# A sketched-attention plus squared-ReLU feed-forward kernel: the first 512 tokens as two chunks of 256, and 256-token chunks in blocks of two w_in tiles

## The chip, the cores and the metric

The kernel runs on one core of one Trainium2 chip. The metric is device microseconds (us) of one execution. Before the change three runs gave 219.83, 217.87 and 219.4 us, a median of 219.4. The core's engines have these names in the profile: PE multiplies matrices (PEld is its loading of weights), DVE, ACT and POOL work on vectors, SP only issues DMAs here. All engines run side by side, each through its own queue in order, and wait for each other at semaphores.

## The reference

Four batches, four heads, 1088 positions, head size 32. The attention is linear: a feature map phi of 64 products replaces the softmax.

```python
def phi(x):
    a = np.einsum('rd,bhsd->bhsr', S1, x)      # r = 8
    b = np.einsum('rd,bhsd->bhsr', S2, x)
    return np.einsum('bhsi,bhsj->bhsij', a, b).reshape(*x.shape[:-1], r * r)
q_p, k_p = (phi(q), phi(k))
kv  = np.einsum('bhsf,bhsd->bhfd', k_p, v)
z   = np.sum(k_p, axis=2)
num = np.einsum('bhsf,bhfd->bhsd', q_p, kv)
den = np.einsum('bhsf,bhf->bhs', q_p, z)[..., None] + 1e-06
x   = (num / den)          # -> (4352 tokens, 128)
h   = np.maximum(x @ w_in, 0.0)       # w_in  (128, 2048)
out = h * h @ w_out                   # w_out (2048, 128)
```

All inputs and the output are float32.

## The kernel before, in words

**Tokens and chunks.** Each batch has 1024 main positions, read as 128 partitions by 8 positions, and 64 remaining ones. The main positions make two groups of 512 tokens (`g` = 0 and 1, four tiles of 128); the remainders of all four batches make one chunk of 256 tokens. So the feed-forward part has nine chunks: eight of 512 tokens and, in seventh place counted from nought, the remainder chunk of 256.

**Attention part of one group.** `proj_t` (line 187) transposes the four heads of a group on PE and evicts them (tile `xt`), `proj` (203) multiplies by the sketches (`ab_ps`, evicted to `ab`) and forms the outer products `ph`, two tiles of 128 tokens at a time (line 221). `Kv` (237) sums keys times values into `kv_ps`, with the remainder's keys last (`finish`, line 263), and evicts the two halves of `kvbd`. For the queries, `feature_t` (295) transposes `ph` in two sets of four (one per pair of heads) and evicts each (`phT`), `numerators` (308) multiplies by `kvbd` into `nd`, `normalize` (319) is a chain of nine DVE instructions from `nd` to `xs` plus one on POOL (`beta`), then transposes on PE (`x_ps`) and an ACT copy to `xT`, float16. `xT` scales each token so that it fits float16, and `beta`, the squared scale, is multiplied in at the end.

**Feed-forward part.** A chunk has 16 blocks, one per tile of 128 columns of `w_in`. A block is: first product `pg` on PE (line 534, float16), ReLU on ACT to `gt` (537), square on DVE to `g2` (538), second product on PE into `po` (554, float32, which PE runs as two instructions). `first_product` runs `LOOK` = 2 blocks ahead of `block`. `pg` has two PSUM buffers. The last chunk (`LAST` = 8) multiplies the other way round (563), so that its tokens need no transposing; each other chunk is transposed back (`o_ps`, 497) and stored by a DMA on SP's queue.

**What sets the order.** `start` (586) is written by hand under `manual_schedule`: every engine runs it in program order. It makes batch 0's keys, its values' sums, the queries of group 0 as far as the first chunk, and the queries of group 1 (`second`, a `q_gen`) as far as their outer products. In it are `idle_products` (150), multiplications of zeros that nothing uses, and the four ACT casts of `w_in` to float16 (616). The remainder's projection `ph_krem[0]` (606) stands ahead of the sums. After `by_hand.close()` the instructions are ordered by a planner, which takes program order as priority and lets later instructions through where earlier ones are not ready by its own costs. Program order there comes from the loop at line 632: after each block `pump(2)` advances up to two lanes of side work (`q_gen`, `k_gen`, remainder), and each `yield n` in a lane says how many blocks it rests. A chunk's first product must come after its `xT` in program order.

Of the kernel before, what the change touches and what calls it, by code (L numbers as in the profile page):

```python
# [8 lines left out]
F32 = mybir.dt.float32  # L9
F16 = mybir.dt.float16  # L10
# [11 lines left out]
def kernel(  # L22
# [11 lines left out]
    nc = tc.nc  # L34

    B, H, S, D = 4, 4, 1088, 32
    DFF, NC = 2048, 16
# [90 lines left out]
    q_sb[1] = load(q, 1, "q_sb")  # L128


    zero = cpool.tile([128, 128], F32)
    nc.vector.memset(zero[:], 0.0)
    iden = cpool.tile([128, 128], F32)
    make_identity(nc, iden[:])
# [12 lines left out]
        nc.vector.memset(_v(v_rem[i], D, [[VW, H]]), 1.0)  # L147
        nc.vector.memset(_v(v_main[i], D, [[VW, H * NJ]]), 1.0)

    def idle_products(n):  # L150
        idle_ps = pspool.tile([128, 512], F32, name="idle_ps", tag="po", bufs=2)
        for i in range(n):
            nc.tensor.matmul(idle_ps[:, 0:128], zero[:, :], zero[:, :])

    idle_products(6)
    w_in = cpool.tile([128, DFF], F16)

    def spread_v(b, eng, j0=0, w=NJ, heads=range(H), pin=False):
# [41 lines left out]
        evict(eng, xt[:, 0 : 128 * n], xt_ps[:, 0 : 128 * n])  # L200
        return xt

    def proj(xt, T, tag, eng, outer, ps_tag="ms", m=32):

        n = 4 if T == 4 else 1
        ab_ps = pspool.tile([128, 256], F32, tag=ps_tag, bufs=2)
        for i in range(n):
            tiled(ab_ps, 64 * i, 64, xt, 128 * i, w_bd[:, :], m=m)
        ab = apool.tile([128, 256], F32, tag="ab", bufs=3)
        if T == 4:  # L210
            evict(
                eng,
                _v(ab, 0, [[16, 4], [64, 4], [1, 16]]),
                _v(ab_ps, 0, [[64, 4], [16, 4], [1, 16]]),
            )
        else:
            evict(eng, ab[:, 0:64], ab_ps[:, 0:64])
        ph = apool.tile([128, 1024], F32, tag=tag, bufs=3)
        for t0 in range(0, T, 2):
            m = min(2, T - t0)  # L220
            outer[(t0 // 2) % len(outer)].tensor_tensor(  # L221
                out=_v(ph, 256 * t0, [[64, 4 * m], [8, 8], [1, 8]]),
                in0=_v(ab, 64 * t0, [[16, 4 * m], [1, 8], [0, 8]]),
                in1=_v(ab, 64 * t0 + 8, [[16, 4 * m], [0, 8], [1, 8]]),
                op=mult,
            )
        return ph

    ph_krem = {}

# [74 lines left out]
        evict(eng, sb[:, 0 : 128 * T], t_ps[:, 0 : 128 * T])  # L305
        return sb

    def numerators(b, phT, m):
        nd = pspool.tile([128, 1024], F32, name="nd", tag="nd", bufs=1)
        for t in range(4):  # L310
# [67 lines left out]
    def chunk_of(b, g, xT, beta):  # L378
        dst = bass.AP(out.tensor, out.offset + (b * S + 4 * g) * E, [[NJ * E, 128], [1, 512]])
        chunks.append((xT, 4, [(beta, 4)], [(dst, 0, 128, 0, 512)]))  # L380

    def x_gen(b, g, phT, m=32):
        nd = numerators(b, phT, m)
# [135 lines left out]
            nc.sync.dma_start(dst, _v(o_sb, c0, [[1, w]], p0, n))  # L519

    LOOK = 2
    LAST = 8
    stream = []
    made = [0]

    def first_product():

        ci, c = divmod(made[0], NC)
        if ci >= len(chunks):
            return False  # L530
        xT, T, _, _ = chunks[ci]
        nt = 128 * T
        pg = pspool.tile([128, 512], F32, tag="pg", bufs=2)
        nc.tensor.matmul(pg[:, 0:nt], w_in[:, 128 * c : 128 * c + 128], xT[:, 0:nt])  # L534
        gt = fpool.tile([128, 512], F32, tag="gt")
        g2 = fpool.tile([128, 512], F32, tag="g2")
        nc.scalar.activation(gt[:, 0:nt], pg[:, 0:nt], Relu)  # L537
        nc.vector.tensor_tensor(  # L538
            out=g2[:, 0:nt], in0=gt[:, 0:nt], in1=gt[:, 0:nt], op=mult
        )  # L540
        stream.append((ci, c, nt, g2))
        made[0] += 1
        return True

    po = [None]
# [1 line left out]
    def block():  # L547
        while len(stream) <= LOOK and first_product():
            pass
        ci, c, nt, g2 = stream.pop(0)  # L550
        if c == 0:
            po[0] = pspool.tile([128, 512], F32, name="po", tag="po", bufs=2)
        if ci < LAST:
            nc.tensor.matmul(  # L554
                po[0][:, 0:nt], w_o[:, 128 * c : 128 * c + 128], g2[:, 0:nt],
                start=(c == 0), stop=(c == NC - 1),
            )
        else:

            for t in range(nt // 128):
                nc.tensor.matmul(  # L563
                    po[0][:, 128 * t : 128 * t + 128],
                    g2[:, 128 * t : 128 * t + 128],
                    w_o[:, 128 * c : 128 * c + 128],
                    start=(c == 0 and t == 0), stop=(c == NC - 1),
                    skip_group_check=True,
                )
        now[0] += 1  # L570
        if c == NC - 1:
# [14 lines left out]
    def start():  # L586
        s_ps = pspool.tile([128, 16], F32, name="s_ps", tag="po", bufs=2)
        xk = [proj_t(k_sb[0], 0, 4, act)]
        nc.tensor.transpose(s_ps[:, :], s_nat[:, :], iden[0:16, 0:16])
        for h in range(H):  # L590
            nc.vector.tensor_copy(
                out=_v(w_bd, 16 * h, [[1, 16]], 32 * h, 32),
                in_=_v(s_ps, 0, [[1, 16]], 32 * h, 32),
            )
        xk.append(proj_t(k_sb[0], 1, 4, act))
        idle_products(2)
        pk = [proj(x, 4, "ph_k", act, (dve,), "pg", m=64) for x in xk]
        idle_products(1)
        xq = proj_t(q_sb[0], 0, 4, act)
        spread_v(0, act, 0, 4)  # L600
        pq = proj(xq, 4, "ph_q", act, (dve,), "pg", m=64)
        xkr = proj_t(k_rm[0], 0, 1, act)
        spread_v(0, act, 4, 4, (0, 1))
        spread_v(0, pool, 4, 4, (2, 3))
        spread_vrem(0, pool)
        ph_krem[0] = proj(xkr, 1, "ph_kr", act, (dve,), "pg", m=64)
        kv0 = Kv(0, 64, "po", 2)
        kv0.tiles(pk[0], 0, range(4))
        pqT = [feature_t(pq, 4, 0, act)]
        kv0.tiles(pk[1], 1, range(4))  # L610
        pqT.append(feature_t(pq, 4, 1, act))
        kv0.finish((dve, dve))
        first = x_gen(0, 0, pqT, 64)
        next(first)
        for c in range(4):
            act.copy(
                w_in[:, 512 * c : 512 * c + 512], w_in32[:, 512 * c : 512 * c + 512]
            )
        for _ in range(3):
            next(first)  # L620
        second = q_gen(0, 1, (dve,), 64)
        next(second)
        idle_products(3)
        next(second)
        idle_products(4)
        whole(first)
        return second

    second = start()
    by_hand.close()  # L630
# [1 line left out]
    for b in range(B):  # L632
# [25 lines left out]
            pump(2)  # L658
        if b + 1 < B:
            drain()  # L660
    for c in range(NC):
        block()
        pump_stores()
        pump(2)
# [31 lines left out]
```

## Time and profile before

| what | value |
|---|---|
| runs | 219.83, 217.87, 219.4 us; median 219.4 |
| the profiled execution | 217.62 us in all, span of its instructions 215.8 us |
| granted PE clock over the span | 0.997 |
| first instruction of the first chunk's first product | 20.15 us |
| DVE busy | 144.3 us (67%) |
| ACT busy | 119.1 us (55%) |
| POOL busy | 44.8 us (21%) |
| squares on DVE, 128x512 | 128 of them, 776 ns mean |
| squares on DVE, 128x256 (remainder chunk) | 16 of them, 424 ns mean |
| ReLU on ACT, 128x512 and 128x256 | 600 and 384 ns mean |

The profile gives each engine's instructions with their start and duration. A matmul's start and end are modelled, and successive matmuls overlap, so that the pitch between two equal ones, not the duration of one, is what one costs. A note in square brackets behind a row is idle time before it and what ended that. Times inside the profile count from the start of the span.

### The profile page before, as it was taken

To read this page: it belongs to the slowest core of one execution; us is meant where nothing else is said; L and a number is where in the kernel's file an instruction comes from. 1 tells how busy PE (TensorE), PEld (TensorE's weight loads), DVE (VectorE), ACT (ScalarE), POOL (GpSimd) and SP (SyncE) were. 2 spreads that over 40 slices of the span, in tenths; PEclk is the share of its full clock that TensorE was granted. 3 is DMA by queue.
4 is the path that set the end of the run, shared out by engine and by line. 5 is a ranking of instruction groups with operands and counts; after the bars stand their busy time and mean duration, and the time that the engine had idled before them with its cause. 6 is when DMAs were issued, how large, how long until landed. Compare 5 with 4: busy or idle time off the path is not lost.

```text
span 215.8 us, 5391 instructions
## 1 busy us (share of the span) xinstructions
PE 207.4 (96%) x2253; PEld 125.4 (58%) x2253; DVE 144.3 (67%) x279; ACT 119.1 (55%) x234; POOL 44.8 (21%) x59
## 2 busy tenths in 40 slices
PE   8889999999999999999999999999999899999992
PEld 7677545445545664655546565455545454669992
DVE  2637696658685799557775567657868777677661
ACT  3655654564566555556466663656465456665550
POOL 1302273004050672004120960013101200000000
PEclk9999999999999999999999999999999999999998
DMA  6999900001000460001000100000000000100001
GB/s 172 270 312 319 267 8 3 2 3 49 3 0 0 131 212 3 3 0 52 2 0 0 52 3 2 3 16 36 2 3 19 30 5 0 49 0 15 12 0 49
DMA packets 13575, 11.35 MB, mean 53 GB/s; under 512 B 3824, under 2 KB 11760, under 8 KB 13552
## 3 DMA queue, kind: packets, MB, share of 16 engines
q1 hardware_dynamic: 12928, 10.95, 17.0%
q8 instruction: 17, 0.28, 0.5%
q10 hardware_dynamic: 624, 0.07, 0.2%
q14 instruction: 6, 0.05, 0.1%
HBM read 8.79 MB, written 2.23 MB: 51 GB/s over the span
## 4 chain that ended last, share of the span: by engine, by line
PE 86%; DVE 6%; ACT 1%; issue 1%; DVEq 0%
PE po L554 46%; PE pg L534 14%; PE po L563 7%; PE nd L180 5%; PE t_ps L299 4%; PE kv_ps L249 3%; PE xt_ps L194 3%; PE ab_ps L180 2%; PE o_ps L497 2%; DVE g L538 1%; DVE xs L358 1%; PE x_ps L370 1%; DVE o_sb L511 1%; DVE small L339 1%; ACT xt L59 1%
## 5 line engine op out<-in xcount | busy, mean ns | idle before, releaser
L538 DVE TENSOR_TENSOR g<-gt 128x512 f32<-128x512 f32 (+1 forms) x144 | 104.8, 737 | 50.5 <-ACT gt L537 48.5
L554 PE MATMUL po<-g,w_o 128*128 128x512 f32 (+1 forms) x256 | 124.1, 570 | 1.1 <-DVE g L538 1.1
L537 ACT ACTIVATE gt<-pg 128x512 f32<-128x512 f32 (+1 forms) x144 | 82.6, 576 | 48.2 <-PE pg L534 47.4
L554 PEld LDWEIGHTS po<-g,w_o 128*128 128x128 f32 x256 | 46.7, 191 | 27.8 <-DVE g L538 9.6
L534 PE MATMUL pg<-xT,w_in 128*128 128x512 f16 x128 | 48.6, 381 | 0.1
L221 POOL TENSOR_TENSOR ph<-ab 128x512 f32<-128x512 f32 (+1 forms) x27 | 32.1, 1213 | 69.7 <-ACT ab L59 69.6
L534 PEld LDWEIGHTS <-w_in 128*128 128x128 f16 x144 | 14.2, 99 | 17.7 <-issue 15.0
L59 ACT COPY sb<-t_ps 128x512 f32<-128x512 f32 (+1 forms) x20 | 10.3, 521 | 12.9 <-PE t_ps L299 12.9
L563 PEld LDWEIGHTS po<-w_o,g 128*128 128x128 f32 x128 | 16.3, 192 | 0.8 <-DVE g L538 0.4
L563 PE MATMUL po<-w_o,g 128*128 128x128 f32 x128 | 16.4, 275 | 0.0
L59 ACT COPY xt<-xt_ps 128x512 f32<-128x512 f32 (+1 forms) x20 | 10.3, 524 | 7.1 <-PE xt_ps L194 7.0
L364 POOL TENSOR_TENSOR beta<-mp 128x4 f32<-128x4 f32 (+1 forms) x10 | 3.1, 319 | 52.3 <-DVE mp L346 44.4
L59 ACT COPY ab<-ab_ps 128x256 f32<-128x256 f32 (+1 forms) x20 | 6.8, 340 | 13.0 <-PE ab_ps L180 12.5
L180 PEld LDWEIGHTS nd<-kvbd,sb 128*32 128x32 f32 (+1 forms) x512 | 8.9, 111 | 7.3 <-issue 3.2
L299 PEld LDWEIGHTS t_ps<-iden,ph 128*128 128x128 f32 x68 | 8.4, 141 | 8.0 <-issue 4.9
L180 PE MATMUL ab_ps<-w_bd,xt 128*32 128x64 f32 (+1 forms) x476 | 11.6, 223 | 1.1 <-ACT xt L59 1.1
L180 PEld LDWEIGHTS ab_ps<-w_bd,xt 128*32 128x32 f32 (+1 forms) x476 | 8.7, 113 | 6.5 <-ACT gt L537 3.0
L180 PE MATMUL nd<-kvbd,sb 128*32 128x66 f32 (+1 forms) x512 | 10.8, 222 | 0.7 <-DVE kvbd L60 0.7
L299 PE MATMUL t_ps<-iden,ph 128*128 128x128 f32 x68 | 10.9, 276 | 0.2 <-DVE ph L221 0.2
L194 PEld LDWEIGHTS xt_ps<-iden,t 128*128 128x128 f32 x52 | 6.4, 141 | 5.2 <-issue 2.8
L194 PE MATMUL xt_ps<-iden,t 128*128 128x128 f32 x52 | 8.3, 276 | 0.1
L249 PEld LDWEIGHTS kv_ps<-v_main,ph 128*32 128x32 f32 (+1 forms) x448 | 5.7, 113 | 2.7 <-issue 0.9
(57 smaller groups left out, 115.6 us busy)
## 6 DMA issues: line engine op xcount, KB each, us to landing
out_dram<-o_sb SPq DMA_DIRECT2D x8, 256.0 KB, 2.0
t<-in_k_dram SPq DMA_DIRECT2D x3, 512.0 KB, 6.5
t<-in_v_dram SPq DMA_DIRECT2D x3, 512.0 KB, 7.5
t<-in_q_dram SPq DMA_DIRECT2D x3, 512.0 KB, 7.3
w_in<-in_moe_w_in_dram SPq DMA_DIRECT2D x2, 512.0 KB, 6.0
k_sb<-in_k_dram SPq DMA_DIRECT2D x2, 256.0 KB, 3.1
q_sb<-in_q_dram SPq DMA_DIRECT2D x2, 256.0 KB, 5.7
v_sb<-in_v_dram SPq DMA_DIRECT2D x2, 256.0 KB, 5.6
```

The lines of the kernel that those rows point to most:

```text
L59: return nc.scalar.copy(dst, src)
L180: nc.tensor.matmul(out_ps[p0 + c : p0 + c + m, c0 : c0 + w], lhsT[:, l0 + c : l0 + c + m], rhs,)
L194: nc.tensor.transpose(xt_ps[:, 128 * i : 128 * i + 128], src[:, w * i + 128 * g : w * i + 128 * g + 128], iden[:, :],)
L221: outer[(t0 // 2) % len(outer)].tensor_tensor(out=_v(ph, 256 * t0, [[64, 4 * m], [8, 8], [1, 8]]), in0=_v(ab, 64 * t0, [[16, 4 * m], [1, 8 ...
L249: nc.tensor.matmul(self.ps[c : c + self.m, VW * pr : VW * pr + VW], _v(ph, c0 + 128 * pr + c, [[1, self.m]], p0, n), _v(vt, v0 + VW * (2 * ...
L299: nc.tensor.transpose(t_ps[:, 128 * t : 128 * t + 128], ph[:, 256 * t + 128 * pr : 256 * t + 128 * pr + 128], iden[:, :],)
L497: nc.tensor.transpose(o_ps[:, 128 * t : 128 * t + 128], oT[:, 128 * t : 128 * t + 128], iden[:, :])
L534: nc.tensor.matmul(pg[:, 0:nt], w_in[:, 128 * c : 128 * c + 128], xT[:, 0:nt])
L537: nc.scalar.activation(gt[:, 0:nt], pg[:, 0:nt], Relu)
L538: nc.vector.tensor_tensor(out=g2[:, 0:nt], in0=gt[:, 0:nt], in1=gt[:, 0:nt], op=mult)
L554: nc.tensor.matmul(po[0][:, 0:nt], w_o[:, 128 * c : 128 * c + 128], g2[:, 0:nt], start=(c == 0), stop=(c == NC - 1),)
L563: nc.tensor.matmul(po[0][:, 128 * t : 128 * t + 128], g2[:, 128 * t : 128 * t + 128], w_o[:, 128 * c : 128 * c + 128], start=(c == 0 and t ...
```

## The change

- The first group of 512 tokens becomes two chunks of 256 (`half_gen`, `half_features_t`). The first half's features are transposed alone, four transposes with one eviction; the second half's are transposed after the four casts of `w_in`, in the hand-written part. The second half's numerators and normalization move out of `start` to the head of the first lane of the loop, with `second` behind them (`rest`).
- `proj` can leave outer products out (`only`); the second half's outer product is issued after the remainder's.
- The remainder's projection stands behind the first half of the keys' sums, no longer ahead of all.
- `kv0.finish` evicts one half of `kvbd` on DVE and one on ACT, where both were on DVE.
- A chunk of 256 tokens takes two tiles of `w_in` in one block: two first products side by side in one `pg`, one ReLU and one square over 512 columns, two second products. This holds for the two new chunks and for the remainder chunk.
- There are ten chunks, so `LAST` is 9; the closing loop runs until nothing is left.
- `zero` is 512 columns wide, and idle products are given by widths: 384+384 in place of six of 128 at the beginning, 256 for two, 128 for one, and one of 384 ahead of the first chunk where there were three and four of 128.

```diff
-    zero = cpool.tile([128, 128], F32)
+    zero = cpool.tile([128, 512], F32)
...
-    def idle_products(n):
+    def idle_products(*widths):
         idle_ps = pspool.tile([128, 512], F32, name="idle_ps", tag="po", bufs=2)
-        for i in range(n):
-            nc.tensor.matmul(idle_ps[:, 0:128], zero[:, :], zero[:, :])
-
-    idle_products(6)
+        for w in widths:
+            nc.tensor.matmul(idle_ps[:, 0:w], zero[:, 0:128], zero[:, 0:w])
+
+    idle_products(384, 384)
...
+    def half_features_t(ph, t0, eng):
+
+        t_ps = pspool.tile([128, 512], F32, name="t_ps", tag="ms", bufs=2)
+        for pr in range(2):
+            for t in range(2):
+                nc.tensor.transpose(
+                    t_ps[:, 256 * pr + 128 * t : 256 * pr + 128 * t + 128],
+                    ph[:, 256 * (t0 + t) + 128 * pr : 256 * (t0 + t) + 128 * pr + 128],
+                    iden[:, :],
+                )
+        sb = apool.tile([128, 512], F32, name="phT_h", tag=f"phT{t0 // 2}")
+        evict(eng, sb[:, :], t_ps[:, :])
+        return [sb[:, 256 * pr : 256 * pr + 256] for pr in range(2)]
...
+    def half_gen(phT, t0, m):
+
+        nd = numerators(0, phT, m, 2)
+        yield 1
+        xT = apool.tile([128, 256], F16, name="xT_h", tag=f"xT_h{t0}", bufs=1)
+        beta = yield from normalize(nd, 2, xT, 0)
+        dst = bass.AP(out.tensor, out.offset + t0 * E, [[NJ * E, 128], [1, 256]])
+        chunks.append((xT, 2, [(beta, 2)], [(dst, 0, 128, 0, 256)]))
+        yield 1
...
-    LAST = 8
+    LAST = 9
...
+        n = 4 // T
         pg = pspool.tile([128, 512], F32, tag="pg", bufs=2)
-        nc.tensor.matmul(pg[:, 0:nt], w_in[:, 128 * c : 128 * c + 128], xT[:, 0:nt])
+        for i in range(n):
+            nc.tensor.matmul(
+                pg[:, nt * i : nt * i + nt],
+                w_in[:, 128 * (c + i) : 128 * (c + i) + 128],
+                xT[:, 0:nt],
+            )
...
-        nc.scalar.activation(gt[:, 0:nt], pg[:, 0:nt], Relu)
-        nc.vector.tensor_tensor(
-            out=g2[:, 0:nt], in0=gt[:, 0:nt], in1=gt[:, 0:nt], op=mult
-        )
+        nc.scalar.activation(gt[:, :], pg[:, :], Relu)
+        nc.vector.tensor_tensor(out=g2[:, :], in0=gt[:, :], in1=gt[:, :], op=mult)
...
+        for i in range(n):
+            c = c0 + i
+            if ci < LAST:
                 nc.tensor.matmul(
+                    po[0][:, 0:nt], w_o[:, 128 * c : 128 * c + 128],
+                    g2[:, nt * i : nt * i + nt],
+                    start=(c == 0), stop=(c == NC - 1),
                 )
...
-        idle_products(2)
+        idle_products(256)
         pk = [proj(x, 4, "ph_k", act, (dve,), "pg", m=64) for x in xk]
-        idle_products(1)
+        idle_products(128)
         xq = proj_t(q_sb[0], 0, 4, act)
         spread_v(0, act, 0, 4)
-        pq = proj(xq, 4, "ph_q", act, (dve,), "pg", m=64)
+        pq = proj(xq, 4, "ph_q", act, (dve,), "pg", m=64, only=(0,))
         xkr = proj_t(k_rm[0], 0, 1, act)
...
-        ph_krem[0] = proj(xkr, 1, "ph_kr", act, (dve,), "pg", m=64)
         kv0 = Kv(0, 64, "po", 2)
         kv0.tiles(pk[0], 0, range(4))
-        pqT = [feature_t(pq, 4, 0, act)]
+        ph_krem[0] = proj(xkr, 1, "ph_kr", act, (dve,), "pg", m=64)
+        outer_of(*pq, 2, dve)
         kv0.tiles(pk[1], 1, range(4))
-        pqT.append(feature_t(pq, 4, 1, act))
-        kv0.finish((dve, dve))
-        first = x_gen(0, 0, pqT, 64)
+        pqT = half_features_t(pq[1], 0, act)
+        kv0.finish((dve, act))
+        first = half_gen(pqT, 0, 64)
         next(first)
...
         for _ in range(3):
             next(first)
+        pqT = half_features_t(pq[1], 2, act)
         second = q_gen(0, 1, (dve,), 64)
         next(second)
-        idle_products(3)
         next(second)
-        idle_products(4)
+        idle_products(384)
         whole(first)
-        return second
+
+        def rest():
+            yield from half_gen(pqT, 2, 64)
+            yield from second
+
+        return rest()
...
-    for c in range(NC):
+    while made[0] < len(chunks) or stream or lanes:
         block()
```

More of the change, by code (lines that the diff above doesn't have):

```diff
@@ L201, in proj_t, with outer_of, proj @@
         return xt
-    def proj(xt, T, tag, eng, outer, ps_tag="ms", m=32):
+    def outer_of(ab, ph, t0, eng, m=2):
+        eng.tensor_tensor(
+            out=_v(ph, 256 * t0, [[64, 4 * m], [8, 8], [1, 8]]),
+            in0=_v(ab, 64 * t0, [[16, 4 * m], [1, 8], [0, 8]]),
+            in1=_v(ab, 64 * t0 + 8, [[16, 4 * m], [0, 8], [1, 8]]),
+            op=mult,
+        )
+    def proj(xt, T, tag, eng, outer, ps_tag="ms", m=32, only=None):
         n = 4 if T == 4 else 1
@@ L218, in proj @@
         ph = apool.tile([128, 1024], F32, tag=tag, bufs=3)
[L219 to L225, printed above, removed]
-            )
-        return ph
+        for t0 in range(0, T, 2) if only is None else only:
+            outer_of(ab, ph, t0, outer[(t0 // 2) % len(outer)], min(2, T - t0))
+        return ph if only is None else (ab, ph)
     ph_krem = {}
@@ L306, in feature_t, with numerators @@
         return sb
-    def numerators(b, phT, m):
+    def half_features_t(ph, t0, eng):
[10 more added lines that the diff above has]
+        return [sb[:, 256 * pr : 256 * pr + 256] for pr in range(2)]
+    def numerators(b, phT, m, T=4):
         nd = pspool.tile([128, 1024], F32, name="nd", tag="nd", bufs=1)
-        for t in range(4):
+        for t in range(T):
             for pr in range(2):
@@ L521 @@
     LOOK = 2
-    LAST = 8
+    LAST = 9
     stream = []
-    made = [0]
+    made = [0, 0]
     def first_product():
-        ci, c = divmod(made[0], NC)
+        ci, c = made
         if ci >= len(chunks):
@@ L532, in first_product @@
         nt = 128 * T
+        n = 4 // T
         pg = pspool.tile([128, 512], F32, tag="pg", bufs=2)
-        nc.tensor.matmul(pg[:, 0:nt], w_in[:, 128 * c : 128 * c + 128], xT[:, 0:nt])
+        for i in range(n):
[3 more added lines that the diff above has]
+                xT[:, 0:nt],
+            )
         gt = fpool.tile([128, 512], F32, tag="gt")
         g2 = fpool.tile([128, 512], F32, tag="g2")
-        nc.scalar.activation(gt[:, 0:nt], pg[:, 0:nt], Relu)
-        nc.vector.tensor_tensor(
-            out=g2[:, 0:nt], in0=gt[:, 0:nt], in1=gt[:, 0:nt], op=mult
-        )
-        stream.append((ci, c, nt, g2))
-        made[0] += 1
+        nc.scalar.activation(gt[:, :], pg[:, :], Relu)
+        nc.vector.tensor_tensor(out=g2[:, :], in0=gt[:, :], in1=gt[:, :], op=mult)
+        stream.append((ci, c, n, nt, g2))
+        made[:] = (ci, c + n) if c + n < NC else (ci + 1, 0)
         return True
@@ L549, in block @@
             pass
-        ci, c, nt, g2 = stream.pop(0)
-        if c == 0:
+        ci, c0, n, nt, g2 = stream.pop(0)
+        if c0 == 0:
             po[0] = pspool.tile([128, 512], F32, name="po", tag="po", bufs=2)
[L553 to L562, printed above, removed]
-                nc.tensor.matmul(
[L564 to L568, printed above, removed]
-                )
+        for i in range(n):
+            c = c0 + i
+            if ci < LAST:
+                nc.tensor.matmul(
+                    po[0][:, 0:nt], w_o[:, 128 * c : 128 * c + 128],
+                    g2[:, nt * i : nt * i + nt],
+                    start=(c == 0), stop=(c == NC - 1),
+                )
+            else:
+                for t in range(nt // 128):
+                    nc.tensor.matmul(
+                        po[0][:, 128 * t : 128 * t + 128],
+                        g2[:, 128 * t : 128 * t + 128],
+                        w_o[:, 128 * c : 128 * c + 128],
+                        start=(c == 0 and t == 0), stop=(c == NC - 1),
+                        skip_group_check=True,
+                    )
         now[0] += 1
-        if c == NC - 1:
+        if c0 + n == NC:
             if ci < LAST:
```

## Prediction

> **What bounds the kernel now.** I read the page first: its busy times, its clock row and its chain of waits.
>
> ```profile
> PE 207.4 (96%) x2253; PEld 125.4 (58%) x2253; DVE 144.3 (67%) x279; ACT 119.1 (55%) x234; POOL 44.8 (21%) x59
> PEclk9999999999999999999999999999999999999998
> PE 86%; DVE 6%; ACT 1%; issue 1%; DVEq 0%
> ```
>
> PE bounds the kernel at full clock. The change takes almost no work from PE: it multiplies the same columns. So the time can only move by what PE spends on nothing useful: the start, where it waits or multiplies zeros, and later bubbles. The start needs the timeline from 14 to 21 us (start, duration, engine, line, operation, count, idle before).
>
> ```profile
> 14.08 0.58 ACT L59 COPY sb<-t_ps 128x512 f32<-128x512 f32 x1 [1.06 <-PE t_ps L299]
> 14.56 2.18 ACT L616 CAST w_in<-w_in 128x512 f16<-128x512 f32 x4
> 15.05 1.16 PE L180 MATMUL nd<-kvbd,sb 128*64 128x66 f32 x32 [0.66 <-DVE kvbd L60]
> 16.84 0.59 ACT L59 COPY xt<-xt_ps 128x512 f32<-128x512 f32 x1
> 17.48 0.69 PE L180 MATMUL ab_ps<-w_bd,xt 128*64 128x64 f32 x16
> 18.09 1.16 PE L153 MATMUL idle_ps<-zero 128*128 128x128 f32 x8
> 18.33 0.69 DVE L358 TENSOR_TENSOR xs<-nd,small 128x512 f16<-128x512 f32 x1
> 19.09 0.40 PE L370 MATMUL x_ps<-iden,xs 128*128 128x128 f16 x4
> 19.52 0.58 ACT L373 COPY xT<-x_ps 128x512 f16<-128x512 f16 x1 [0.89 <-PE x_ps L370]
> 20.15 0.59 PE L534 MATMUL pg<-xT,w_in 128*128 128x512 f16 x2
> ```
>
> Two chains meet at 19.1: the numerators and nine DVE instructions (15.05 to 19.02), and ACT's queue: casts, `xt`, then PE's `ab_ps` and the idle products that stand before `x_ps`. The reader is to see that they are level, so that shortening one alone gains nothing. Third, the table of stretches behind the first chunk's beginning (PE, PEld, DVE, ACT, POOL busy, clock, DMA).
>
> ```profile
> 24.00:26.00 2.00, 2.00 (x22) 1.20 (x24) 0.42 (x1) 1.56 (x3) 0.00 (x0) 1.00 1.10 258
> 30.00:32.00 2.00, 1.99 (x39) 0.76 (x27) 1.93 (x6) 0.89 (x2) 1.71 (x4) 1.00 0.00 0
> 32.00:34.00 2.00, 1.85 (x53) 0.78 (x49) 2.00 (x3) 0.81 (x2) 2.00 (x2) 1.00 0.00 0
> ```
>
> DVE is full from 28 to 34 us, while POOL forms batch 1's outer products: normalization and squares share DVE. PE looks busy, but the chain of waits runs over DVE from 27.05 to 32.56 (5.5 us); PE's work in it, four first products, three second and 0.85 of side work by pitch, is 4.9. So 0.6 us is lost, hidden by modelled ends.
>
> **The change part by part.**
>
> *The start of PE.* `zero` quadruples. DVE memsets of 64 and 128 columns took 0.112 and 0.165 us, 0.83 ns a column, so 512 take 0.48, 0.32 longer, and PE's first product (1.05) waits for it. The columns multiplied stay the same (768, at a pitch of 0.21 per 128x128 instruction in the cold clock). The key transposes at 3.79 follow directly, and `s_ps` at 4.80 had waited 0.33 anyway, which takes up some. I carry +0.2; bounds 0 (all taken up) and +0.5 (memset at four times 0.165).
>
> *The keys' sums.* PE waited 0.38 us at 10.57 for the remainder's `xt`. Moved behind the first sums, this wait goes: they start at 10.2 instead of 10.74. Forward, by the chain's pieces: sums 0.91, remainder product 0.34, sums 1.05, one set of transposes 0.59 (two before), remainder's sums 0.38: 13.47, plus 0.2. DVE isn't late: its outer products of 0.67 each run on to 12.1, and as the remainder's `ab` comes at 11.8, its 0.41 and the postponed 0.67 end at 12.9, before the second half's transposes ask for them. ACT evicts the features until 13.9, then one half of `kvbd`; a 64-partition ACT copy is not shown, the 128x64 one took 0.21: bounds 0.2 and 0.37 (128x256), I take 0.23. So the numerators start at 14.25, not 15.05, and the casts at 14.14, not 14.56.
>
> *To the first product.* The DVE chain: 16 numerators 0.6, then 2.77 minus about half of the two wide steps (reduction 0.56, `xs` 0.69): `xs` would stand at 17.2. ACT's queue has got longer instead: the second half's eviction goes between the casts and `xt`, at a pitch of 0.54. Against before, `xt` comes at -0.42+0.54: `ab_ps` starts at 17.60. PE then has 0.58 of products and one idle product of 384 columns (two instructions of 0.32, against eight of 0.107), then `x_ps` at 18.82. Two transposes instead of four bring `xT`'s copy at 19.15; 256 columns took 0.37 (`ab`), 512 take 0.58. First product: 19.57, against 20.15: **-0.58**. The normalization's gain of 1.8 us is covered by ACT's and PE's queues. Bounds: -1.0 (no delay of PE's start, idle product free) and -0.1 (memset +0.5, another eviction's 0.17).
>
> *Work that moves behind it.* The second half's 16 numerators (0.58) are ready when PE waits for `xT` from 19.0 to 19.57: hidden; without that cover +0.58. Two more `x_ps` 0.11, and the two feature transposes that PE did in its hole at 19.68, 0.22: **+0.33**.
>
> *Blocks of two tiles.*
>
> ```profile
> 41.81 0.38 PE L534 MATMUL pg<-xT,w_in 128*128 128x512 f16 x1
> 42.88 0.38 PE L534 MATMUL pg<-xT,w_in 128*128 128x512 f16 x1
> ...
> 187.50 0.27 PE L534 MATMUL pg<-xT_rem,w_in 128*128 128x256 f16 x1
> 188.04 0.27 PE L534 MATMUL pg<-xT_rem,w_in 128*128 128x256 f16 x1
> ```
>
> A 512-column block has a pitch of 1.073 us, a 256-column one at best 0.546. A pair costs 1.092, so the 16 pairs of the first group **+0.30** (bounds 0 and 0.5). The remainder chunk gains: nine of its blocks from 187.50 to 192.73 took 0.581 each, as ACT (0.38) and DVE (0.43) answered too late; paired, ReLU and square take 0.60 and 0.69 per 1.09 of PE. 16x0.581-8x1.092 = 0.56: **-0.56** (bounds -0.9 and 0).
>
> Here stands a rule that speaks against the pairs. The Trainium skill, "TensorE: Matmul & The Clock Gate", section "Back-to-back issue gap", adds about 2.5 ns to each warm matmul, whatever its width. A pair has three instructions more than a block of 512, which would be 7.5 ns a pair, 0.12 us for 16, where the rows' pitches make it 0.30.
>
> *Normalizations in the loop.* DVE gets one more chain: about 2.2 us, plus one more `o_sb`. The second half's chunk is appended after block 5 and asked for at block 6; between PE has seven blocks and 2.2 us of side work, 9.8 us, while from numerators to `xT` a chain took 7.4 in the steady part (173.35 to 180.80) and 10.6 in the crowded one (25.84 to 36.40): 0, at worst +0.8. Its DVE work begins before POOL's outer products do, so that I give back 0.2 of the 0.6 lost there: **-0.2** (bounds -0.6 and +0.3). Group 1 is now six blocks later: numerators after block 8, chunk appended after block 13, asked for at block 14, behind only six blocks and 1.9 us of side work, 8.4 us less the wait for `kvbd` (about 0.7). A chain of 7.4 fits but for queueing, one of 10.6 makes PE wait 2.9. POOL's outer products should be over by then, so the steady row is nearer: **+0.4** (bounds 0 and 2.9). Behind that wait stand second products of blocks 14 and 15 on PE, and ACT and DVE starve with it.
>
> *Queues.* SP issues one store more, of two half size, to a queue whose loads for batch 2 wait for buffers that come free as before. POOL gets one `beta` more (0.3). Both lie beside PE's work. The side work of later batches, one block a step, keeps its places.
>
> Sum: -0.58+0.33+0.30-0.56-0.2+0.4 = -0.3. The profiled execution took 217.62 (span 215.8), so 217.3; it lies 1.8 under the median of the runs, 219.4, against which I predict **219.1**.
>
> **The rivals.**
>
> 1. *Slower: group 1 comes late.* The planner lets six blocks pass between numerators and first product; if the chain takes 10.6 as in the first stage, PE waits 2.9 rather than 0.4: 221.6. For: DVE has 5.5 us of squares and 3.9 of other work in 10 us. Against: POOL, whose copies and outer products stretched DVE's squares there (three in 3.42 us), has done most by then. From 8.4 us on (7.7 of cover, and the 0.7 that the other terms gain), the kernel is slower than before.
>
> 2. *Slower: the clock falls.* The removed idle products leave PE idle from about 16.0 to 17.6. In the trace, gaps of up to 0.7 us (at 9.25) left the clock full; transposes in the cold start took 0.421 us, warm ones 0.272. If the clock fell for as long as it took to rise (1.05 to about 6), half of 5 us would be lost: 221.6.
> The Trainium skill, same page, section "Why this matters for your kernels", asks for no idle gap over about 3 us; by it 1.6 us would cost nothing, and the sum would stand. No row of before has such a gap.
>
> 3. *Faster: the first chunk starts with `xs`.* If ACT's casts, eviction and `xt` ran quicker than I chain them, the 17.2 of the normalization would count, the first product would come near 18, and the time 217.5. Against: each ACT step is in program order and has its duration in a row.
>
> 4. *Nothing comes out at all,* because PE's queue after the start holds the same work. This is inside my forecast: the sum is 0.3.
>
> **How the numbers follow.** My forecast 0.68; group 1 late by over 2 us 0.12; clock 0.05; early first product 0.10; the planner disturbing later stages, either sign, 0.05. About 1% (2.2 us) is what a measurement can tell from no change: the runs of before alone spread over 2.0. The forecast's own range, from its bounds and that spread, is 217.5 to 220.6; reaching into rivals 1 and 3, 216.8 to 221.2. Faster by over 1% (under 217.2) needs rival 3 in full: 0.09. Slower (over 221.6) needs rivals 1 or 2 beyond their centres, or both: 0.12. Within 1%: 0.79.
>
> **What would show it.** Numerators near 14.25, casts near 14.14, first product near 19.6: the start. If `x_ps` comes right after `xs`, rival 3. A remainder chunk of eight blocks at 1.09: the pairs. A wait of PE for `xT`, or DVE, at the change from the second half to group 1: rival 1. A granted clock below 1.00 between 16 and 22 us: rival 2. I am wrong if PE's idle products and waits before 20 us were not the only thing that moved, above all if the planner orders a later stage otherwise.

## The result, and the profile after

The changed kernel took a median of 216.26 us (215.65 to 217.08, 20 runs), the kernel before 217.75 (217.09 to 220.69, 20 runs). The ratio, taken by rounds, is 0.9925, with a 95% interval of 0.9903 to 0.9946: 0.75% faster. Ratios leave out slow executions, those more than 1.5% above the fastest of the same kernel, while medians and ranges are of all. I had forecast 219.1, with a range from 216.8; the result lies 0.5 below the range. The three runs of before that I had (219.83, 217.87, 219.4) hold two of the five longest of its 20.

The profiled execution of the changed kernel took 216.98 in all, its span 215.2, at a granted clock of 1.0. Its page, in the rows shown of before:

```profile
PE 206.1 (96%) x2279; PEld 130.3 (61%) x2279; DVE 143.2 (67%) x280; ACT 118.5 (55%) x229; POOL 43.9 (20%) x60
PEclk9999999999999999999999999999999999999999
PE 93%; DVE 3%; ACT 1%; issue 1%; DVEq 0%
```

PE has 26 more records: more of the pairs' narrower products, fewer idle ones. What has moved is the last row: the chain of waits runs over PE for 93% of the span instead of 86%, and over DVE for 3% instead of 6%. The timeline of the start (start, duration, engine, line, operation, count, idle before):

```profile
14.65 2.18 ACT L650 CAST w_in<-w_in 128x512 f16<-128x512 f32 x4
14.67 0.69 PE L180 MATMUL nd<-kvbd,phT_h 128*64 128x66 f32 x16 [0.56 <-ACT kvbd L59]
...
17.14 0.42 DVE L374 TENSOR_TENSOR xs<-nd,small 128x256 f16<-128x256 f32 x1
17.33 0.59 ACT L59 COPY xt<-xt_ps 128x512 f32<-128x512 f32 x1
17.98 0.69 PE L180 MATMUL ab_ps<-w_bd,xt 128*64 128x64 f32 x16
18.59 0.91 PE L153 MATMUL idle_ps<-zero 128*128 128x384 f32 x2
19.34 0.28 PE L386 MATMUL x_ps<-iden,xs 128*128 128x128 f16 x2
19.65 0.37 ACT L389 COPY xT_h<-x_ps 128x256 f16<-128x256 f16 x1 [0.52 <-PE x_ps L386]
20.31 0.60 PE L563 MATMUL pg<-xT_h,w_in 128*128 128x256 f16 x4
```

`xs` is ready at 17.56, but `x_ps` comes at 19.34: ACT's eviction (`xt`), PE's `ab_ps` and the idle product of 384 columns lie between. By the clock of the span the first product is even later than before (20.31, not 20.15). That is misleading: the first sketch product already lies 0.71 later. Half of it, 0.36, is there at the first eviction (5.27 against 4.91), behind the wider `zero`; the rest is PE's full speed, which came later in this execution. So I count from the first sketch product (`ab_ps`, A), which is 6.57 in before and 7.28 here. From the PE rows of each trace I work out five stages: A to the first first product (B), B to the first second product of batch 1's first chunk, from there to that of batch 3's first chunk, and from there to the end of the last second product.

| kernel | A at | A to B | B to batch 1 | batch 1 to 3 | batch 3 to end | A to end |
|---|---|---|---|---|---|---|
| before | 6.57 | 13.59 | 47.26 | 94.37 | 50.10 | 205.32 |
| after | 7.28 | 13.04 | 47.36 | 94.36 | 49.32 | 204.08 |
| after, profiled again | 7.24 | 12.88 | 47.42 | 94.36 | 49.31 | 203.97 |
| forecast of the difference | +0.2 | -0.78 | +0.83 | 0 | -0.56 | -0.51 |

(The forecast's terms, put into stages: -0.58 holds the +0.2 of PE's later start; +0.83 is 0.33+0.30-0.2+0.4.) The first profile of after had the first of A's products still at half speed, 0.17 of its 13.04.

The stretches behind the start, in the columns of the table shown of before (PE, PEld, DVE, ACT, POOL busy, clock, DMA):

```profile
24.00:26.00 2.00, 2.00 (x41) 1.48 (x40) 1.86 (x7) 0.67 (x2) 0.19 (x1) 1.00 0.01 4
30.00:32.00 2.00, 2.00 (x43) 1.63 (x44) 0.96 (x1) 0.96 (x3) 2.00 (x3) 1.00 0.03 8
```

DVE's crowded stretch has gone apart: the normalization runs at 24 to 26 us (1.86 of 2.00), and at 30 to 32, while POOL is full, DVE is busy for 0.96 instead of 1.93. The remainder chunk:

```profile
188.26 0.38 PE L563 MATMUL pg<-xT_rem,w_in 128*128 128x256 f16 x2
189.35 0.38 PE L563 MATMUL pg<-xT_rem,w_in 128*128 128x256 f16 x2
```

A pair has a pitch of 1.085 (four of them from 187.18 to 191.52), and no wait stands between. Before, there was one more loss behind this chunk, at the last chunk's first second product:

```profile
194.02 0.79 PE L534 MATMUL pg<-xT,w_in 128*128 128x512 f16 x2
194.65 1.95 PE L563 MATMUL po<-w_o,g 128*128 128x128 f32 x16
```

The two first products take 0.43 by pitch, so the second product came 0.2 late; it waited for a square on DVE.

### The profile page after: what moved, and what is told of

Read it like the earlier page. It is cut to its first block, busy times and chain, and to the rows that moved or that the text cites. A ratio compares the mean times of both kernels' runs of the same rounds, so it can differ in the third digit from the quotient of the medians.

```text
span 215.2 us, 5435 instructions
## 1 busy us (share of the span) xinstructions
PE 206.1 (96%) x2279; PEld 130.3 (61%) x2279; DVE 143.2 (67%) x280; ACT 118.5 (55%) x229; POOL 43.9 (20%) x60
## 4 chain that ended last, share of the span: by engine, by line
PE 93%; DVE 3%; ACT 1%; issue 1%; DVEq 0%
PE po L587 48%; PE pg L563 15%; PE po L597 7%; PE nd L180 5%; PE xt_ps L194 4%; PE ab_ps L180 4%; PE kv_ps L251 3%; PE t_ps L301 3%; PE idle_ps L153 2%; PE o_ps L523 2%; PE x_ps L386 1%; ACT xt L59 1%; DVE g L571 1%; DVE xs L374 1%; DVE o_sb L537 1%
## 5 line engine op out<-in xcount | busy, mean ns | idle before, releaser
L571 DVE TENSOR_TENSOR g<-gt 128x512 f32<-128x512 f32 x136 | 104.1, 773 | 50.6 <-ACT gt L570 49.2
L570 ACT ACTIVATE gt<-pg 128x512 f32<-128x512 f32 x136 | 81.3, 599 | 48.4 <-PE pg L563 47.1
L587 PEld LDWEIGHTS po<-g,w_o 128*128 128x128 f32 x288 | 52.4, 191 | 23.4 <-DVE g L571 6.9
L563 PE MATMUL pg<-xT,w_in 128*128 128x512 f16 x112 | 42.5, 381 | 0.0
L59 ACT COPY sb<-t_ps 128x512 f32<-128x512 f32 (+1 forms) x18 | 9.2, 515 | 11.2 <-PE t_ps L301 11.2
L380 POOL TENSOR_TENSOR beta<-mp 128x4 f32<-128x4 f32 (+2 forms) x11 | 2.6, 239 | 61.9 <-DVE mp L362 61.8
L180 PEld LDWEIGHTS nd<-kvbd,sb 128*32 128x32 f32 x480 | 7.9, 109 | 5.7 <-issue 2.4
L180 PE MATMUL nd<-kvbd,sb 128*32 128x66 f32 x480 | 9.6, 222 | 0.1
L301 PE MATMUL t_ps<-iden,ph 128*128 128x128 f32 x60 | 9.3, 273 | 0.0
L204 DVE TENSOR_TENSOR ph<-ab 128x512 f32<-128x512 f32 (+1 forms) x9 | 5.7, 686 | 4.6 <-ACT ab L59 4.6
```

The source lines that it names most:

```text
L59: return nc.scalar.copy(dst, src)
L180: nc.tensor.matmul(out_ps[p0 + c : p0 + c + m, c0 : c0 + w], lhsT[:, l0 + c : l0 + c + m], rhs,)
L204: eng.tensor_tensor(out=_v(ph, 256 * t0, [[64, 4 * m], [8, 8], [1, 8]]), in0=_v(ab, 64 * t0, [[16, 4 * m], [1, 8], [0, 8]]), in1=_v(ab, 64 ...
L301: nc.tensor.transpose(t_ps[:, 128 * t : 128 * t + 128], ph[:, 256 * t + 128 * pr : 256 * t + 128 * pr + 128], iden[:, :],)
L563: nc.tensor.matmul(pg[:, nt * i : nt * i + nt], w_in[:, 128 * (c + i) : 128 * (c + i) + 128], xT[:, 0:nt],)
L570: nc.scalar.activation(gt[:, :], pg[:, :], Relu)
```

## The experiments

The theory: the start gains what was forecast, the remainder's pairs gain somewhat more, and the stage between them pays back most of its added work, because the second group's normalization comes later and no longer falls on POOL's outer products. The rival for that stage: the two halves themselves bring it, wherever DVE does them. Medians are of 12 runs each unless said, with the median of before measured beside it and the ratio with its interval. About 0.5 us of a time is uncertain, so that the stages decide smaller questions.

### The remainder's pairs alone

This is the kernel before with the changed kernel's `first_product`, `block` and closing loop; `LAST` stays 8.

```diff
+        n = 4 // T
         pg = pspool.tile([128, 512], F32, tag="pg", bufs=2)
-        nc.tensor.matmul(pg[:, 0:nt], w_in[:, 128 * c : 128 * c + 128], xT[:, 0:nt])
+        for i in range(n):
+            nc.tensor.matmul(
+                pg[:, nt * i : nt * i + nt],
+                w_in[:, 128 * (c + i) : 128 * (c + i) + 128],
+                xT[:, 0:nt],
+            )
...
-    for c in range(NC):
+    while made[0] < len(chunks) or stream or lanes:
```

> The kernel before with only one part of the change: the remainder chunk in eight blocks of two w_in tiles; start and first chunk as before. Theory A (the remainder's pairs are worth more than the 0.56 us forecast): from the beginning of its first product to the first second product of the last chunk the stage is 0.8 us shorter, span 215.0, ratio to before 0.996. Rival B (the whole difference comes from the start): no change, ratio 1.000. My forecast's own term: -0.56 us, ratio 0.9975.

216.94 against 217.46, ratio 0.9985 (0.996 to 1.001). By stages only the last moved: 49.32 against 50.10, -0.78, all others within 0.07. The pairs are worth 0.78 from batch 3 to the end, though the interval of the time alone doesn't tell it from nought.

### The change without the remainder's pairs

```diff
-        n = 4 // T
+        n = 1 if ci == LAST - 1 else 4 // T
+        w = n * nt
...
-        nc.scalar.activation(gt[:, :], pg[:, :], Relu)
-        nc.vector.tensor_tensor(out=g2[:, :], in0=gt[:, :], in1=gt[:, :], op=mult)
+        nc.scalar.activation(gt[:, 0:w], pg[:, 0:w], Relu)
+        nc.vector.tensor_tensor(out=g2[:, 0:w], in0=gt[:, 0:w], in1=gt[:, 0:w], op=mult)
```

> The kernel after with the remainder chunk back in 16 blocks of one tile; the rest of the change stays. Theory A: about half of the gain is left, ratio to before 0.996 to 0.997. Rival B: nearly all is left, 0.993. If the start and the first stage gave nothing, as the two profiles laid side by side at 57 us suggest (0.26 us later after the change), the ratio is 1.001.

217.72 against 217.46, ratio 1.0006 (0.9985 to 1.0027). The last stage is back at 50.10 to the hundredth, and the others are those of after (12.87, 47.30, 94.36). From A to the end this kernel is 0.69 shorter than before (204.63), which its time doesn't show. The scatter of the start, told below, is as large as that.

### Before, its second group six blocks late

```diff
+    def late(gen):
+        yield 6
+        yield from gen
+
-    second = start()
+    second = late(start())
```

> The kernel before, with group 1's lane resting six blocks before its first step, so that its normalization falls behind POOL's outer products as it does after the change; nothing else. Theory A (the crowding of DVE from 27 to 33 us cost 0.6 us, and the change took it away): PE's chain no longer runs over DVE there; the tenth block or so comes 0.6 us earlier, a wait of 0.3 us at the change to group 1 comes in its place: net 0 to -0.5 us, ratio 0.998. Rival, my forecast's term (being late costs 0.4 and relieves only 0.2): +0.2 us or more, ratio 1.001 and up to 1.01 if the chain stretches.

218.59 against 217.46, ratio 1.0044 (1.0025 to 1.0063): slower, by 0.58 from A to the end. This run missed its question. One long rest made the lane of batch 0's remainder come in earlier than in either kernel, and PE waited for POOL's outer product:

```profile
29.39 0.33 PE L299 MATMUL t_ps<-iden,ph 128*128 128x128 f32 x1 [1.20 <-POOL ph L221]
```

Without these 1.20 it would have been shorter than before. It shows only that an order with a hole in it is dear, so I repeated it with the slots taken.

### Before, its second group late, with the slots taken

```diff
+    def late(gen):
+        for n in (1, 1, 1, 2, 1):
+            yield n
+        yield from gen
+
-    second = start()
+    second = late(start())
```

> The kernel before with group 1's lane resting six blocks, now by five steps that take a slot of the pump each, as the second half's do after the change, so that the remainder's lane is not let through earlier (in the first try PE waited 1.2 us for POOL's outer product of the remainder, 1.42 us by the pitch of its instructions). Theory A (before the change PE lost 0.28 and 0.42 us to a crowded DVE at 24 and 26 us after the first sketch product, which the later normalization takes away): the stretch from the first second product to that of group 1's chunk is 23.9 us instead of 24.34, without a wait for POOL, ratio 0.998. Rival (the relief comes from the halves themselves, not from the lateness): 24.3 to 24.7, ratio 1.000 or over.

217.19 against 217.40, ratio 0.9995 (0.9964 to 1.0025). From A to batch 1 it takes 60.42 against 60.85: lateness alone *gains* 0.43. The chains of waits at 30 to 33 us say why (start, duration, what). Before:

```profile
30.98 0.69 DVE xs L358
31.67 0.84 DVE g L538
32.56 1.12 PE po L554 x2
```

With the second group late:

```profile
31.12 0.44 PE t_ps L299 x4
31.56 0.70 PE kv_ps L249 x57
32.26 0.32 PE pg L534
```

Before, PE's second product waits for a square that stands behind `xs` on DVE and takes 0.84 beside POOL's outer products. Late, the chain holds nothing but PE. So for the stage, lateness, which I had priced as a cost, is a gain.

### The change, its second group no longer behind the second half

```diff
-        def rest():
-            yield from half_gen(pqT, 2, 64)
-            yield from second
-        return rest()
+        return half_gen(pqT, 2, 64), second
...
+            add_work(half)
         add_work(second if b == 0 else q_gen(b, 1, (pool,)))
...
-            pump(2)
+            pump(3 if b == 0 else 2)
```

> The kernel after, with the second half and group 1 in lanes of their own and three lanes advanced a block in the first loop, so that group 1's normalization comes as early as before, together with POOL's outer products. Theory A: DVE is full again from about 24 to 33 us and the gain of that stage goes back: 0.4 to 0.8 us slower than the kernel after, ratio to before 0.995 to 0.997. Rival (the order of the lanes is without effect, or lateness was what cost): same as after, 0.9925, or up to 0.3 us faster.

216.25 against 217.46, ratio 0.9946 (0.9927 to 0.9965): as fast as after. From A to batch 1 it takes 60.26, after 60.30 (the second profile) and 60.40. I had expected a loss of 0.4 to 0.8. The crowding did come back:

```profile
31.32 1.13 PE L587 MATMUL po<-g,w_o 128*128 128x256 f32 x4 [0.63 <-DVE g L571]
```

By pitch PE loses 0.90 there. But with the second group early, PE's wait at the change to it is gone (0.28), as are some 0.3 at its numerators, 0.11 ahead of B and smaller pieces. So lateness isn't what the change needs to gain: two orders with different waits give the same sum. Here the rival was right.

### The remainder's projection ahead of the sums again

```diff
+        ph_krem[0] = proj(xkr, 1, "ph_kr", act, (dve,), "pg", m=64)
         kv0 = Kv(0, 64, "po", 2)
         kv0.tiles(pk[0], 0, range(4))
-        ph_krem[0] = proj(xkr, 1, "ph_kr", act, (dve,), "pg", m=64)
```

> The kernel after with the remainder's projection ahead of the first half's sums again, as before the change; nothing else. Forecast's step (PE waited 0.38 us there for ACT, and the sums started 0.54 us late): first product 0.4 to 0.55 us later after the first sketch product, 13.3 to 13.4 instead of 12.87; ratio to before 0.995. Rival (the numerators wait for ACT's eviction of the features and of kvbd, which the wait does not move): first product at 12.9, ratio as after.

217.02 against 217.55, ratio 0.9974 (0.9956 to 0.9992); after, measured beside it, 216.48, 0.9945 (0.9925 to 0.9965). From A to B 13.32 against 12.88: +0.44. The numerators of after, and then of this kernel:

```profile
14.47 0.69 PE L180 MATMUL nd<-kvbd,phT_h 128*64 128x66 f32 x16 [0.56 <-ACT kvbd L59]
```

```profile
14.85 0.69 PE L180 MATMUL nd<-kvbd,phT_h 128*64 128x66 f32 x16 [0.56 <-ACT kvbd L59]
```

Counted from A (7.24 and 7.16), they come 0.46 later, and the first product 0.44 later: the wait for the remainder's `xt` goes through to the end of the start, as the prediction had it.

### Without the idle product ahead of the first chunk

```diff
-        idle_products(384)
         whole(first)
```

> The kernel after without the idle product of 384 columns ahead of the first chunk. Theory A (it stands in PE's queue ahead of x_ps while xs has long been ready, so it lies on the path): the first product comes 0.64 us earlier after the first sketch product, 12.25 instead of 12.87 us, and 0.3 to 0.6 us of it reach the end, as the second half's numerators then lose some of their cover; ratio to before 0.990. Rival (the eviction of group 1's sketch products on ACT stands ahead of xT anyway and holds it): 0.1 us or nothing. Second rival (PE's clock falls without it): products at half pitch behind 18 us, ratio above 0.995.

216.41 against 217.40 (215.28 to 217.6), ratio 0.9956 (0.9925 to 0.9988). From A to B 12.25 against 12.88: -0.63, about the 0.64 of its two instructions. From A to the end 203.45, 0.52 less than after. Yet the median is no better. Six of the 12 runs had a mean granted clock of 0.988 to 0.992; they took 216.39 to 217.6. The six at 0.997 to 1.0 took 215.28 to 216.43. The profiled run was one at 1.0, so no trace shows where in the kernel the clock fell. So the idle product buys the clock in some executions, and pays for it with 0.6 in all.

### Idle products in narrow pieces

```diff
-    zero = cpool.tile([128, 512], F32)
+    zero = cpool.tile([128, 128], F32)
...
-    idle_products(384, 384)
+    idle_products(*[128] * 6)
...
-        idle_products(256)
+        idle_products(128, 128)
...
-        idle_products(384)
+        idle_products(128, 128, 128)
```

> The kernel after with zero 128 columns wide and every idle product in pieces of 128 again, the same columns in all. Theory A (the wide memset of 0.48 us costs PE's start 0.40 us, and the first eviction comes 0.36 us later for it): PE starts at 1.05 us, the first eviction at 4.91 instead of 5.27; of the time, 0.2 to 0.4 us less than the kernel after, ratio to before 0.991. Rival (when PE's products become fast is set by a clock that does not know the kernel's start, and the loss is taken up before): start of the sketch products at the same place on average, ratio as after, 0.9925 to 0.994.

216.67 against 217.40, ratio 0.9948 (0.9911 to 0.9985): not to be told from after. PE's first product starts at 1.05 again, so the wide `zero` had cost 0.40 there, and A is at 5.95. But the keys for batch 1 then come 0.27 late for PE, and 0.50 is lost in the middle stage (94.87), where the profile names no waker:

```profile
135.67 0.23 PE L386 MATMUL x_ps<-iden,xs 128*128 128x128 f16 x1 [0.32 <-issue]
```

By its pitch this transposition comes 0.49 late; the idle time in the note is less, as the end of the one before it is modelled.

### The casts spread, no idle product

The zeros are narrow, as above; two casts come later in ACT's order, and the idle product ahead of the first chunk is gone.

```diff
-        for c in range(4):
+
+        def cast(c):
             act.copy(
...
+
+        cast(0)
+        cast(1)
         for _ in range(3):
             next(first)
         pqT = half_features_t(pq[1], 2, act)
         second = q_gen(0, 1, (dve,), 64)
         next(second)
+        cast(2)
         next(second)
-        idle_products(384)
+        cast(3)
```

> The kernel after, with only two of the four casts of w_in ahead of the second half's eviction, the third behind group 1's first eviction and the fourth behind its second, where ACT waits for PE; without the idle product of 384 columns; and with the narrow zero. Theory A (the chain to the first product is ACT's queue, no longer the normalization): first product 11.2 us after the first sketch product instead of 12.87, of which 0.8 to 1.5 us reach the end; ratio to before 0.987. Rival (what comes earlier at the first product is lost behind it, to DVE or to the casts): ratio 0.991 to 0.993, as after.

217.14 against 217.40, ratio 0.9967 (0.9932 to 1.0001). ACT's queue was shortened: `x_ps` comes 10.29 after A (17.10 less 6.81), in after 12.06 (19.34 less 7.28). The first product didn't follow, as something new was in front of it:

```profile
19.58 0.63 PE L194 MATMUL xt_ps<-iden,t 128*128 128x128 f32 x4 [1.57 <-DMA t<-in_k_dram]
```

Batch 1's keys hadn't arrived, and their transposes stand ahead of the first product in PE's order. So the next limit of the start is a transfer. Six of its runs had a granted clock of 0.992 or less, as without the idle product above.

### The best start I could put together

On top of the spread casts:

```diff
+    k_sb[1] = load(k, 1, "k_sb")
     w_o = cpool.tile([128, DFF], F32)
...
-    k_sb[1] = load(k, 1, "k_sb")
...
+        idle_products(128, 128, 128, 128, 128)
         cast(2)
```

> The kernel after with three edits: two of the four casts of w_in moved into gaps of ACT behind group 1's evictions; narrow zero; and batch 1's keys loaded ahead of w_out, since in the try before PE waited 1.57 us for them at 18 to 19.6 us, as the planner sets their transposes ahead of the first first product. Idle products stay, but five of 128 columns ahead of group 1's sketch products, where PE waits, and none ahead of the first chunk. Theory A (the start's end is set by ACT's queue, and behind that by the arrival of batch 1's keys): no wait for a DMA, first product 11.6 to 11.9 us after the first sketch product, against 12.87; 0.8 to 1.2 us less than the kernel after, ratio to before 0.987 to 0.989. Rival (w_out, now 1.6 us later, makes the first second product wait, or DVE gives the gain back): ratio 0.992 or above.

216.52 against 217.55, ratio 0.9952 (0.9933 to 0.9972). The keys are loaded ahead of `w_out`, and PE's idle time is filled before `ab_ps`, where it costs nothing. From A to B 12.00, 0.88 less than after, with all granted clocks at 0.998 or more. But the middle stage lost 1.08 (95.44), most of it in one place:

```profile
135.43 0.59 PE L587 MATMUL po<-g,w_o 128*128 128x512 f32 x1 [0.91 <-issue]
```

PE stands still between the two instructions of one float32 product, whose operands are there, with no waker that the profile shows.

### The same with fewer instructions

```diff
-    zero = cpool.tile([128, 128], F32)
+    zero = cpool.tile([128, 256], F32)
...
-    idle_products(*[128] * 6)
+    idle_products(256, 256, 256)
...
-        idle_products(128, 128)
+        idle_products(256)
...
-        idle_products(128, 128, 128, 128, 128)
+        idle_products(256, 256)
```

> The start of the last combination (two casts of w_in in gaps of ACT, batch 1's keys ahead of w_out, no idle product ahead of the first chunk) with fewer idle instructions: zero 256 columns wide, idle products of 256, two of them ahead of group 1's sketch products. In that combination the first stage gained 0.87 us and lost 1.07 at one place at 135 us, where PE waited 0.91 us for nothing that the profile shows, between the two halves of one product; the planner's order behind the first fifth is the same as in the kernel after. Theory (that wait hangs on where PE's instruction stream stands, 18 instructions further than in the kernel after; here 4): no such wait, first product 12.0 us after the first sketch product, 0.8 to 0.9 us less than the kernel after from there on, ratio to before 0.990 to 0.991. Rival (the earlier start itself brings that wait about): the wait stays, ratio 0.9945 as the kernel after.

215.06 (214.44 to 215.69, 6 runs) against 217.44, ratio 0.9883 (0.9854 to 0.9913). It beats both kernels: its longest run is about the shortest of after (215.65). From A to B 11.74, and the middle stage is back at 94.36. It pays 0.5 of that at once: with the keys first, `w_out` comes late, and PE's first second product waits 0.47 for it. From A to the end it takes 203.44, 0.53 less than after. The rest of its lead lies ahead of A (5.71), which one profile can't settle.

### The change once more

> The kernel after once more, beside its variants on the same chip. From the profiles, stage by stage: 1.4 us less than before from the first sketch product on, ratio 0.9925 to 0.9945. Its profile tells whether the late rise of PE's speed in the first profile (first sketch product at 7.28 us, at half pitch for 0.17 us) was chance: if so, the first sketch product stands between 6.1 and 7.4 us; if the wide zero and its later start cause it, at 7.2 to 7.4 again.

216.48 against 217.55, ratio 0.9945 (0.9925 to 0.9965). Its stages agree with the first profile's but for the 0.17 at A, which makes the stage lengths good to about 0.1. Its A, at 7.24, fits both answers of the expectation; the kernels with the same start that had A at 6.14 and 6.23 show that the wide `zero` alone doesn't bring the late rise about.

## Why the prediction was wrong

The forecast was 219.1 and the result 216.26, 2.84 lower. It falls into two parts.

**The base: 1.65.** The step that failed most is the last one of the sum: "it lies 1.8 under the median of the runs, 219.4, against which I predict 219.1". I set the sum on a median of three runs. Over 20 runs the median is 217.75; the profiled execution (217.62), on which the whole working stood, was typical. From it the forecast would have been 217.3, inside 1.1 of the result. The forecast of "within 1%" was right, but the range was centred on a number that the profile had not supported.

**The sum: 1.2.** It gave -0.3 where the medians give -1.5. By stages:

- *The start: right.* Forecast -0.78 from A to B, measured -0.55 in the first profile and -0.71 in the second. Its parts held too: the remainder's projection goes through with 0.44, and `xs` waits on ACT's and PE's queues, as the first fence above shows. Rival 3 (the first chunk starts with `xs`) is out for this kernel; the spread casts show that it takes a change of ACT's order, and then a transfer bounds.
- *PE's later start: mis-sized, and below the scatter.* Forecast +0.2, at PE's first product it is 0.40 (1.45 against 1.05), near the bound of 0.5. Across the profiles A lies between 6.14 and 7.28 with the wide `zero`, between 6.19 and 6.81 with before's start.
- *Blocks of two tiles: right.* Forecast +0.30 for 16 pairs. By the pitch of 1.085 against 1.074 it is 16 x 0.011 = 0.18. The Trainium skill, "TensorE: Matmul & The Clock Gate", section "Back-to-back issue gap", gives an estimate of 0.12; the measurement lies between the two.
- *Normalizations in the loop: this term failed, in sign.* Forecast -0.2+0.4 = +0.2. The stage from B to batch 1 grew by 0.10 (0.16 in the second profile); less the 0.18 of the pairs and the 0.33 of the moved work, about -0.4 is left. The moved work wasn't measured by itself, so the split between the two terms rests on its price. What was wrong shows in before: I counted the second group's lateness only by PE's wait at the change of chunks. That wait is there, 0.28 at 46.8 us. But the same lateness takes the normalization off POOL's stretch, where PE had waited for squares; in before, lateness alone gains 0.43 net. I had seen 0.6 lost there, and gave back 0.2 of it. (PE's work that I listed for that stretch adds to 4.3, not 4.9; its side work there was nearly 1.5, not 0.85. The 0.6 stands: PE's waits between 27.05 and 32.56 are 0.18, 0.10 and 0.33 by pitch.) Nor is lateness the only way: the crowded order of the changed kernel comes to the same sum. So whether lateness or the halves themselves took the 0.4 in the changed kernel stays open.
- *The remainder: mechanism right, size off.* Forecast -0.56, measured -0.78, alone and undone alike. I had counted 16 blocks against eight pairs, and not the change to the last chunk: before, its first second product came late behind a square on DVE, by about 0.2.

From A to the end the sum of all was forecast at -0.51 and measured at -1.24 and -1.35. Of the -1.5 of the medians some 0.2 are left for what lies ahead of A, where I expected +0.2; the scatter of A is larger than both.

**The rivals.** Group 1 late by 2.9: no, the wait is 0.28, since POOL's work is over by then, as argued against it. The clock: not in the changed kernel, whose 20 runs had 0.996 or more; it does fall in half of the runs without the idle product, so the rival's mechanism exists, and in this kernel the product of 384 that the change leaves there keeps it away. Nothing comes out: no.

## What to carry to other kernels

Set a forecast on the profiled execution that its terms come from, and let a few other runs only widen the range. Where two engines' long pieces fall together (here DVE's normalization and POOL's outer products), moving one of them later can gain more than the wait that it makes at the other end, so price both ends, not only the deadline. In before that alone was worth 0.43; in the changed kernel another order did as well. After each shortening of a start ask which transfer is next: here the keys of the next batch, and behind them `w_out`.

## What the runs showed of the hardware

**PE's full speed begins at a time of its own.** After's start, and below it that of the best kernel:

```profile
4.17 1.06 PE L194 MATMUL xt_ps<-iden,k_sb 128*128 128x128 f32 x4
...
6.28 1.06 PE L153 MATMUL idle_ps<-zero 128*128 128x256 f32 x2
7.28 1.32 PE L180 MATMUL ab_ps<-w_bd,xt 128*64 128x64 f32 x32
```

```profile
3.90 0.69 PE L194 MATMUL xt_ps<-iden,k_sb 128*128 128x128 f32 x4
...
5.71 1.15 PE L180 MATMUL ab_ps<-w_bd,xt 128*64 128x64 f32 x32
```

The same four transposes take 1.06 or 0.69. In after the speed doubles only within the sketch products, at 7.68 us, in the other kernel at 4.08. The kernel without the remainder's pairs, whose start is after's instruction for instruction, had A at 6.23. So A moves by more than 1 us among executions. The granted clock's row reads 1.00 all through it, but only because the trace has no record of the clock ahead of the rise: its first record begins at 7.68 and 7.13 in the two profiles of after, at 6.13 in before, at 4.68 and 4.85 in the two kernels with after's start and A at 6.14 and 6.23. In 13 of the 14 profiles this record lasts 208.2 us (in one 211.6) and the half clock that follows begins behind the last product. So a mean of 0.996 in a profiled run cost nothing, and a mean of 1.000, where the record lasts to the end of the span, says that the rise came late. Of after's 32 runs the 14 at 1.000 had a median of 216.66, the other 18 one of 215.99: by this reading the long runs are mostly those with the late rise.

**The granted clock can fall without the idle product.** In the kernel without the idle product PE waits 1.32 us at 17.5, and six of 12 runs had a clock of 0.988 to 0.992. Of 98 runs of after and its variants with some idle products between the transposes of `q_sb` at 15.8 us and `x_ps` none was below 0.996. The wait of 1.32 is in after too, followed by the idle product; which stretch of idleness counts stays open. Nor do idle products there always keep the clock: before has seven, and 8 of its 110 runs beside the variants were at 0.977 to 0.992.

**PE can stand still with nothing to wait for.** 0.91 us in the best start with narrow zeros, 0.50 with narrow zeros alone, none with fewer, wider instructions, though the code of the middle stage is the same in all three. That a place in the instruction stream matters would fit, and the traces support it: both standstills come ahead of PE's 1,748th matmul, which is a second product in one kernel and a transposition in the other. In both a transfer of 16 KB on the queue that the profile calls "instruction" had ended 1.2 to 1.5 us before (at 133.97 and 134.44). But after has such transfers without a standstill (one ends at 135.73), and no run changed the place alone, so the cause stays open.
